# Reordering stage one of a gated attention and mixer block: values' rows loaded later, the first MLP normalisation moved into `w1` of block 3, two of block 3's subtractions on VectorE

## The chip, the cores and the metric

The kernel runs on one core of a Trainium2 chip. The metric is the device time of one execution in microseconds. Engines are named as the profile names them: PE is TensorE's matmul, PEld its weight load, DVE is VectorE, ACT is ScalarE, POOL is GpSimd and SP is SyncE, which does nothing here but issue DMAs. A suffix q (SPq, ACTq) marks the issue of a DMA by that engine's queue.

## The reference

Everything is float32, for one sequence of 2048 tokens of width 448, 16 heads of width 28.

```python
g = sigmoid((x * gate_w).sum(-1, keepdims=True))
a = attention(x, wq, wk, wv, wo)      # 16 query heads of 28, one key and one value head
h  = gelu(layernorm(x) @ w1)          # token mixing, on whole rows
hs = shift(h) @ w2                    # the four quarters of h, moved by -1, +1, -2, +2 tokens
x1 = x + hs
b  = x1 + gelu(layernorm(x1) @ w3) @ w4
out = g * a + (1 - g) * b
```

## The kernel before

The 2048 tokens are four blocks of 512 (`b` = 0 to 3), and a block is four tiles of 128 tokens (`t` = 0 to 3). A float32 product is made of three matmuls on reduced-precision halves: a tensor `raw` is split into a high part (a copy that rounds, on ACT) and a low part (`raw` minus the high part, on DVE or POOL). The kernel has three stages: projections, token mixing and `w2` (stage one, roughly the first 136 us); the channel MLP `w3`, `w4`; attention. The change lies in stage one and moves one small piece to its end.

The order of the work is written out by hand: each engine runs its instructions in the order in which the Python code emits them, and each waits only for its own operands and buffers. So a wait on an engine holds up all that was emitted behind it for that engine. All engines but ACT's few stores leave their DMAs to SP's queue, in that same way in order. A DMA takes one of eight semaphores in turn, and its issue waits until the former user of that semaphore has landed; SP's and ACT's DMAs share the eight.

For one block, stage one does this:

- `stage_w1(b)`: four times 11 matmuls into a PSUM bank of `mm1` (four banks in turn), GELU on ACT into `hf`, a caller's extra work `between(t)`, and a 32x32 transpose on DVE into `ht`. Then SP stores `ht` as `hd` in DRAM with four DMAs.
- `read_h(b)`: two SP DMAs read `hd` back as `hr`, with channels on the partitions (first the quarters 2 and 3, then 0 and 1).
- `split_h(b)`: for the quarters `m` in the order 2, 0, 1, 3, ACT copies `hr` into `hh` and POOL subtracts into `hl`. After quarter 2, `carry_h(b)` issues seven small SP DMAs that move rows of that quarter to the 16 spare partitions of the others. At the end POOL copies the two edge columns into the block before.
- `stage_w2(b)`: per tile 11 matmuls into one of two banks `hs`, then DVE adds the bank to the residual `x1`. With two banks, the third tile's matmuls start when the first tile's addition is done.
- `stage_q(u)`: one group of four query heads; PE projects, ACT copies to `qf` and stores it to `qd` by its own queue. The queries' spare rows hold keys and values as well, so `stage_kv(b)` reads the values' rows of a block from `qd` into `vT` with two SP DMAs. `vT` is used first by `stage_v`, in the middle of `stage_w2(3)`.

The channel MLP needs the normalised block 0: `stats_tile` (DVE) gives mean and variance of a row of `x1`, `stats_end` (POOL) the reciprocal root, `layernorm_norm` (DVE) one subtraction and multiplication into `xn` and a transpose into `xt4`; `xt_write` stores that as `xd` with four SP DMAs, `xt_read` loads it as `xr` with three, and `ln_split` (ACT, then DVE) splits it. `load_w34(i)` loads the raw weights of the channel MLP, two DMAs each.

Three buffers of 8 KB a partition, tag `raw`, serve in turn for `ht`, `hr`, `xn4` and `xt4`. In the kernel before the turn gives `xt4` the buffer that `ht` of block 3 had. The order of the last part of stage one before the change can be read at the end of the functions printed here.

Of the kernel before, what the change touches and what calls it, by code (L numbers as in the profile page):

```python
# [9 lines left out]
F32 = mybir.dt.float32  # L10
F32R = mybir.dt.float32r
AF = mybir.ActivationFunctionType
ALU = mybir.AluOpType
# [3 lines left out]
P = 128  # L17
S = 2048
D = 448
# [4 lines left out]
NB = S // 512  # L24
NT = S // P
NF = F // P
NE = D // 32
# [10 lines left out]
def f32(ap):  # L38
    return ap.bitcast(F32)
# [3 lines left out]
def gated_mix_kernel(  # L43
# [12 lines left out]
    nc = tc.nc  # L56
# [80 lines left out]
    def stats_tile(pool, b, t, mv):  # L137
        st = pool.tile([P, 6], F32, tag="st", bufs=2, name=f"st_{pool.name}_{b}_{t}")
        nc.vector.bn_stats(st, x1[:, 4 * b + t, :])
        nc.vector.bn_aggr(mv[:, t, :], st)  # L140

    def stats_end(mv, rs):
        nc.gpsimd.tensor_tensor(rs, mv[:, :, 1], epst, ALU.add)
        nc.gpsimd.tensor_tensor(rs, rs, powt, ALU.pow)

    def stats_tiles(pool, b):
        return (pool.tile([P, 4, 2], F32, tag="mv", bufs=2, name=f"mv_{pool.name}_{b}"),
                pool.tile([P, 4], F32, tag="rs", bufs=2, name=f"rs_{pool.name}_{b}"))
# [8 lines left out]
    def layernorm_norm(b, t, mv, rs, xn, xt4):  # L157
        xt = x1[:, 4 * b + t, :]
        nc.vector.tensor_scalar(xn, xt, mv[:, t, 0:1], rs[:, t:t + 1], op0=ALU.subtract, op1=ALU.mult)
        nc.vector.transpose(xt4[:, :, t, :], xn.rearrange("p (f j) -> p f j", j=32))  # L160
# [3 lines left out]
    def xt_write(b, xt4):  # L164
        xd_of[b] = dram.tile([NE, 32, 4, 128], F32, tag="xd", bufs=2, name=f"xd_{b}")
        for p in range(4):
            nc.sync.dma_start(xd_of[b][:, :, p].rearrange("f i u -> i f u"),
                              xt4[32 * p:32 * p + 32].rearrange("i f t j -> i f (t j)"))

    def xt_read(b, raw):  # L170
        xd = xd_of.pop(b)
        nc.sync.dma_start(raw[:, 0:3, :], xd[0:12].rearrange("(c f) i p u -> (f i) c (p u)", c=3))
        for k in (0, 64):
            nc.sync.dma_start(raw[k:k + 64, 3, :], xd[12:14].rearrange("f i p u -> (f i) (p u)"))
# [75 lines left out]
    with tc.tile_pool(name="s1b", bufs=1) as s1b, \  # L250
            tc.tile_pool(name="ps1", bufs=1, space=PSUM) as ps1:
        s1_stack = ExitStack()
        s1 = s1_stack.enter_context(tc.tile_pool(name="s1", bufs=1))
        turn = [0]

        def mm1(name):
            k = turn[0] % 4
            turn[0] += 1
            return mm_tile(name) if k < 2 else ps1.tile([P, 512], F32, tag="tp", bufs=2, name=name)
# [62 lines left out]
        def rest(g, n, b):  # L322
            cols = slice(512 * b, 512 * b + 512)
            return qd[g].rearrange("(j c) s -> j c s", c=32)[0:n // 4, DH:32, cols]

        def stage_kv(b):
            for g in range(2):
                at = 32 * b + 16 * g
                nc.sync.dma_start(vT[at:at + 16, :], rest(2 + g, 16, b))
# [69 lines left out]
        def carry_h(b):  # L399
            src = f32(hl[b])  # L400
            for i, (low, m, _) in enumerate(CARRY):
                o = 2 + SHIFTS[m]
                to = f32((hl if low else hh)[b])[C:P, m, o:o + 512]
                nc.sync.dma_start(to, src[16 * i:16 * i + 16, 2, 0:512])  # L404

        hd_of, hr_of = {}, {}

        def stage_w1(b, between=None):
            ah, al = xact[b]
            rs = rs1_of.pop(b)[1]  # L410
            ht = s1.tile([P, 4, 512], F32, tag="raw", bufs=3, name=f"ht_{b}").rearrange("p c n -> p (c n)")
            ht = ht[:, 0:4 * D].rearrange("p (f t j) -> p f t j", f=NE, t=4)
            for t in range(4):
                ps = mm1(f"h_{b}_{t}")[:, 0:D]
                tok = slice(t * P, (t + 1) * P)
                for c in range(3):
                    nc.tensor.matmul(ps, ah[:, c, tok], w1h[:, c, :], start=(c == 0), stop=False)
                    nc.tensor.matmul(ps, al[:, c, tok], w1h[:, c, :], start=False, stop=False)
                    nc.tensor.matmul(ps, ah[:, c, tok], w1l[:, c, :], start=False, stop=False)
                nc.tensor.matmul(ps, ah[:, 3, tok], w1h[:, 3, :], start=False, stop=False)  # L420
                nc.tensor.matmul(ps, ah[:, 3, tok], w1l[:, 3, :], start=False, stop=True)
                hf = s1.tile([P, 512], F32, tag="hf", bufs=3, name=f"hf_{b}_{t}")[:, 0:D]
                nc.scalar.activation(hf, ps, AF.Gelu_apprx_tanh, scale=rs[:, t:t + 1])
                if between:
                    between(t)
                nc.vector.transpose(ht[:, :, t, :], hf.rearrange("p (f j) -> p f j", j=32))
            hd = hd_of[b] = dram.tile([NE, 32, 4, 128], F32, tag="hd", bufs=2, name=f"hd_{b}")
            for p in range(4):
                nc.sync.dma_start(hd[:, :, p].rearrange("f i u -> i f u"),
                                  ht[32 * p:32 * p + 32].rearrange("i f t j -> i f (t j)"))  # L430
# [8 lines left out]
        def split_h(b):  # L439
            hh[b] = s1b.tile([P, 4, 516], F32R, tag="hh", bufs=2, name=f"hh_{b}")  # L440
            hl[b] = s1b.tile([P, 4, 516], F32R, tag="hl", bufs=2, name=f"hl_{b}")
            hr = hr_of.pop(b)
            for tt in (hl, hh):
                if b == 0:
                    nc.gpsimd.memset(f32(tt[b])[0:C, :, 0:2], 0.0)
                else:
                    nc.gpsimd.tensor_copy(tt[b][0:C, :, 0:2], f32(tt[b - 1])[0:C, :, 512:514])
            for m in ORDER:
                raw = hr[0:C, m, :].rearrange("n (p t j) -> n p t j", p=4, t=4)
                hi, lo = [tt[b][0:C, m, 2:514].rearrange("n (t p j) -> n p t j", p=4, t=4) for tt in (hh, hl)]  # L450
                nc.scalar.copy(hi, raw)
                nc.gpsimd.tensor_tensor(lo, raw, f32(hi), ALU.subtract)
                if m == 2:
                    carry_h(b)
            for tt in (hh, hl):
                if b:
                    nc.gpsimd.tensor_copy(tt[b - 1][0:C, :, 514:516], f32(tt[b])[0:C, :, 2:4])
                if b == NB - 1:
                    nc.gpsimd.memset(f32(tt[b])[0:C, :, 514:516], 0.0)

        def stage_w2(b, between=None):
            for t in range(4):
                ps = hs_tile(f"hs_{b}_{t}")[:, 0:D]
                for m in range(4):
                    o = 2 + t * P + SHIFTS[m]
                    nc.tensor.matmul(ps, hh[b][0:C, m, o:o + P], w2h[0:C, m, :], start=(m == 0), stop=False)
                    nc.tensor.matmul(ps, hh[b][:, m, o:o + P], w2l[:, m, :], start=False, stop=False)
                    if m != 2:
                        nc.tensor.matmul(ps, hl[b][:, m, o:o + P], w2h[:, m, :], start=False, stop=(m == 3))
                xt = x1[:, 4 * b + t, :]  # L470
                nc.vector.tensor_add(xt, xt, ps)
                if between:
                    between(t)
# [66 lines left out]
        stage_w1(1, second)  # L540
        split_h(0)
        read_h(1)
        stage_kv(0)
        stage_kv(1)
        stage_w1(2, lambda t: ln1_tile(3, t))
        split_h(1)
        read_h(2)
        stage_kv(2)
        stage_q(12)
        stage_q(13)  # L550
        stage_w2(0)
        mv0, rs0 = stats_tiles(s1, "m")

        def fourth(t):
            if t == 0:
                split_h(2)
            stats_tile(s1, 0, t, mv0)

        stage_w1(3, fourth)
        read_h(3)  # L560
        stats_end(mv0, rs0)
        xn4 = s1.tile([P, 2048], F32, tag="raw", bufs=3, name="xn4")[:, 0:4 * D].rearrange("p (t n) -> p t n", t=4)
        xt4 = s1.tile([P, 2048], F32, tag="raw", bufs=3, name="xt4")[:, 0:4 * D].rearrange(
            "p (f t j) -> p f t j", f=NE, t=4)
        stage_w2(1, lambda t: layernorm_norm(0, t, mv0, rs0, xn4[:, t, :], xt4))
        xt_write(0, xt4)
        split_h(3)
        stage_q(14)
        stage_q(15)
        stage_kv(3)  # L570
        s1_stack.close()

        late = ctx.enter_context(tc.tile_pool(name="late", bufs=1, side="right", reuse_waits="tile"))
# [57 lines left out]
        xraw2[0] = big("xr_0").rearrange("p (c n) -> p c n", c=4)  # L631
        load_w34(0, s2a)
        xt_read(0, xraw2[0])

        def third(t):
            if t == 3:
                ln_split(0, 0, 2)
# [16 lines left out]
    with tc.tile_pool(name="s2", bufs=1, reuse_waits="tile") as s2, \  # L654
# [47 lines left out]
        for b in range(NB):  # L702
            acc = [ps2.tile([P, 512], F32, tag="acc", bufs=4, name=f"acc_{b}_{t}") for t in range(4)]
            gs = {}
            for f in range(NF):
                if f == 9 and b + 1 < NB:
                    mv, rs = layernorm_stats(s2a, b + 1)
                if f == 10 and b + 1 < NB:
                    xt4 = big(f"xt4_{b + 1}")[:, 0:4 * D].rearrange("p (f t j) -> p f t j", f=NE, t=4)
                if f in (10, 11) and b + 1 < NB:  # L710
                    for t in (2 * f - 20, 2 * f - 19):
                        xn = s2a.tile([P, 512], F32, tag="xn", bufs=1, name=f"xn_{b + 1}_{t}")[:, 0:D]
# [474 lines left out]
```

## Time and profile before

| | |
|---|---|
| median of 3 runs | 924.17 us (923.05 to 924.31) |
| the profiled execution's own time | 923.91 us |
| its span, first to last instruction | 922.1 us |
| PE busy in the span | 905.3 us (98%) |
| DVE, ACT, POOL busy | 541.1, 632.2, 107.0 us |
| mean granted TensorE clock | 0.991 of full speed |
| DMA share in slices 3 to 6 of 40 (46 to 138 us) | 6, 5, 6 and 5 tenths |

Times of single instructions below are microseconds from the start of the span. The parts of the page are averages over three stages with different limits; what this change is worth is read from the stretch of 60 to 140 us alone, in the timeline of each engine. In a row of a timeline stand the start, the duration, the engine, the line, the operation, the tiles (buffer numbers left out), and, in brackets, how long the engine had been idle before it and what ended that.

### The profile page before, as it was taken

What the parts mean: (1) busy time and instruction counts of PE and PEld (TensorE: products, weight loads), DVE (VectorE), ACT (ScalarE), POOL (GpSimd) and SP (SyncE); (2) the same over time, 40 slices, a digit from 0 to 9 for tenths busy, and PEclk for the clock granted to TensorE, in tenths of its full rate; (3) what the DMA queues carried; (4) which work ended last, traced back from release to release, by engine and by line L of the source; (5) the groups of instructions that cost most, each with busy time, mean ns of one, the idle gap of its engine ahead of it and who ended that gap; (6) DMA issues with size and microseconds to landing.
All of it is one profiled execution on the core that took longest, in us unless ns stands there. A gap on an engine that the chain in (4) does not pass through costs nothing.

```text
span 922.1 us, 24138 instructions
## 1 busy us (share of the span) xinstructions
PE 905.3 (98%) x10097; PEld 649.7 (70%) x10097; DVE 541.1 (59%) x1083; ACT 632.2 (69%) x1135; POOL 107.0 (12%) x140
## 2 busy tenths in 40 slices
PE   9999879999999999999999999999999999999998
PEld 7898768888888888885556655556655656665554
DVE  4653344542344655536666666676666666666775
ACT  5433135522222122239999999999999999999996
POOL 3134300112100052002200000000000000000000
PEclk9999879999999999999999999999999999999999
DMA  9865654140041141111000001100011000010001
GB/s 302 304 156 146 150 181 129 44 96 22 9 98 36 38 98 52 46 30 59 15 14 25 26 14 44 35 26 26 3 36 56 21 8 26 14 51 18 15 14 43
DMA packets 50608, 58.23 MB, mean 63 GB/s; under 512 B 9616, under 2 KB 35008, under 8 KB 50496
## 3 DMA queue, kind: packets, MB, share of 16 engines
q1 hardware_dynamic: 47328, 50.95, 20.1%
q10 hardware_dynamic: 3168, 5.70, 1.7%
q8 instruction: 80, 1.31, 0.6%
q14 instruction: 32, 0.26, 0.1%
HBM read 39.80 MB, written 15.59 MB: 60 GB/s over the span
## 4 chain that ended last, share of the span: by engine, by line
PE 92%; DMA 3%; DVE 2%; SPq 1%; ACT 1%; issue 1%; POOL 0%; ACTq 0%; DVEq 0%; POOLq 0%
PE bank L985 24%; PE bank L948 22%; PE bank L849 7%; PE acc L699 5%; PE acc L698 5%; PE acc L700 5%; PE g L132 4%; PE g L131 4%; PE g L133 4%; PE g L134 1%; PE g L135 1%; DMA hr<-hd 1%; SPq L404 1%; PE q L309 1%; DMA xr<-xd 1%; PE q L131 1%
## 5 line engine op out<-in xcount | busy, mean ns | idle before, releaser
L975 ACT ACTIVATE p<-bank 128x512 f32<-128x512 f32 x762 | 386.9, 617 | 1.5 <-PE bank L948 1.5
L985 PE MATMUL bank<-p,vext 128*32 128x256 f32 x3076 | 244.4, 379 | 0.0
L985 PE MATMUL bank<-pd,vext 128*32 128x256 f32 x1020 | 241.1, 380 | 0.0
L972 DVE COPY pd<-bank 128x512 f32<-128x512 f32 x254 | 175.3, 692 | 51.2 <-PE bank L948 49.9
L985 PEld LDWEIGHTS bank<-p,vext 128*32 128x32 f32 x3076 | 126.7, 110 | 81.6 <-ACT p L975 0.5
L687 ACT ACTIVATE gh<-g 128x512 fp32r<-128x512 f32 x54 | 32.2, 597 | 183.1 <-PE g L135 183.1
L989 DVE TENSOR_TENSOR o<-o,bank 128x256 f32<-128x256 f32 x222 | 93.5, 421 | 92.1 <-ACT p L975 53.9
L980 ACT ACTIVATE pd<-pd 128x1024 f32<-128x1024 f32 x127 | 141.0, 1110 | 0.0
L948 PE MATMUL bank<-qh,kH 30*128 30x512 f32 x1024 | 116.7, 444 | 0.0
L985 PEld LDWEIGHTS bank<-pd,vext 128*32 128x32 f32 x1020 | 112.4, 110 | 0.1
L690 DVE TENSOR_TENSOR gl<-gf,gh 128x512 fp32r<-128x512 f32 x54 | 37.2, 689 | 119.4 <-ACT gf L688 119.3
L948 PE MATMUL bank<-qh,kL 28*128 28x512 f32 x1024 | 103.8, 391 | 0.0
L948 PE MATMUL bank<-ql,kH 28*128 28x512 f32 x1024 | 103.7, 391 | 0.0
L948 PEld LDWEIGHTS bank<-qh,kH 30*128 30x128 f32 x1024 | 60.4, 183 | 57.2 <-ACT p L975 45.9
L699 PE MATMUL acc<-w4l,gh 128*128 128x448 f32 x216 | 79.0, 366 | 0.0
L698 PE MATMUL acc<-w4h,gh 128*128 128x448 f32 x216 | 78.9, 365 | 0.0
L700 PE MATMUL acc<-w4h,gl 128*128 128x448 f32 x216 | 78.8, 365 | 0.0
L849 PE MATMUL bank<-wof,on 128*32 128x224 f32 x1008 | 73.1, 367 | 0.0
L132 PE MATMUL g<-al,w3h 128*128 128x512 f32 x168 | 65.8, 392 | 0.0
L131 PE MATMUL g<-ah,w3h 128*128 128x512 f32 x168 | 65.7, 391 | 0.0
L133 PE MATMUL g<-ah,w3l 128*128 128x512 f32 x168 | 65.6, 390 | 0.0
L948 PEld LDWEIGHTS bank<-ql,kH 28*128 28x128 f32 x1024 | 50.8, 186 | 9.5
(201 smaller groups left out, 1170.3 us busy)
## 6 DMA issues: line engine op xcount, KB each, us to landing
qd<-qf ACTq DMA_DIRECT2D x16, 256.0 KB
qm<-qd SPq DMA_DIRECT2D x16, 256.0 KB
qr<-qd SPq DMA_DIRECT2D x16, 256.0 KB
rb<-rd SPq DMA_DIRECT2D x15, 256.0 KB
x<-in_x_dram SPq DMA_DIRECT2D x4, 896.0 KB
hd<-ht SPq DMA_DIRECT2D x16, 224.0 KB
hr<-hd SPq DMA_DIRECT2D x8, 448.0 KB
xd<-xt SPq DMA_DIRECT2D x16, 224.0 KB
```

Source lines behind the costliest of these rows:

```text
L131: nc.tensor.matmul(ps, wh[:, c, :], ah[:, c, :], start=(c == 0), stop=False)
L132: nc.tensor.matmul(ps, wh[:, c, :], al[:, c, :], start=False, stop=False)
L133: nc.tensor.matmul(ps, wl[:, c, :], ah[:, c, :], start=False, stop=False)
L698: nc.tensor.matmul(ps, gh[:, tok], w4h[i][:, k, :], start=(f == 0), stop=False)
L699: nc.tensor.matmul(ps, gh[:, tok], w4l[i][:, k, :], start=False, stop=False)
L700: nc.tensor.matmul(ps, gl[:, tok], w4h[i][:, k, :], start=False, stop=(f == stop))
L849: nc.tensor.matmul(ps[32 * j:32 * j + 32, cols], on_of[u][:, tok], wof[:, u % NG, cols], start=start, stop=stop, tile_position=(0, 32 * j))
L948: nc.tensor.matmul(bs[j], w, a, start=(i == 0), stop=(i == 2), tile_position=(32 * j, 0))
L972: nc.vector.tensor_copy(ps[j], bs[j])
L975: behind[kt % 2] = nc.scalar.activation(ps[j], bs[j], AF.Exp, scale=SCALE)
L980: ins = nc.scalar.activation(pd, pd, AF.Exp, scale=SCALE)
L985: nc.tensor.matmul(pv[32 * j:32 * j + 32, q], vext[:, kt, :], p_of[u, kt][j][:, q], start=start, stop=stop, tile_position=(0, 32 * j))
```

## The change

Four things are moved, and one is shared:

- `stage_kv(0)`, `(1)` and `(2)` are issued together behind `read_h(2)`, and `stage_kv(3)` behind `xt_read(0)`.
- The statistics of block 0's rows of `x1` are taken in `stage_w2(0)`, each behind its addition, and not in `stage_w1(3)`.
- The normalisation of block 0 runs in `stage_w1(3)`, ahead of each tile's transpose of `hf`, and not in `stage_w2(1)`. Its `xn` takes buffers of the tag `qf` (four of 2 KB); its `xt4` is allocated together with `ht` of block 3, so that it gets the buffer that `hr` of block 1 had. `xn4` is gone.
- `xt_write(0)` is issued right behind the stores of `hd` of block 3, ahead of `read_h(3)`.
- In `split_h(3)` the subtractions of quarters 0 and 3 run on DVE, those of 2 and 1 stay on POOL.

```diff
-        def stage_w1(b, between=None):
+        def token_tile(b):
+            ht = s1.tile([P, 4, 512], F32, tag="raw", bufs=3, name=f"ht_{b}").rearrange("p c n -> p (c n)")
+            return ht[:, 0:4 * D].rearrange("p (f t j) -> p f t j", f=NE, t=4)
+
+        def stage_w1(b, between=None, ht=None):
...
-                nc.gpsimd.tensor_tensor(lo, raw, f32(hi), ALU.subtract)
+                eng = nc.vector if b == NB - 1 and m in (0, 3) else nc.gpsimd
+                eng.tensor_tensor(lo, raw, f32(hi), ALU.subtract)
...
         read_h(1)
-        stage_kv(0)
-        stage_kv(1)
         stage_w1(2, lambda t: ln1_tile(3, t))
         split_h(1)
         read_h(2)
-        stage_kv(2)
+        for b in range(3):
+            stage_kv(b)
         stage_q(12)
         stage_q(13)
-        stage_w2(0)
         mv0, rs0 = stats_tiles(s1, "m")
+        stage_w2(0, lambda t: stats_tile(s1, 0, t, mv0))
+        stats_end(mv0, rs0)
 
         def fourth(t):
             if t == 0:
                 split_h(2)
-            stats_tile(s1, 0, t, mv0)
-
-        stage_w1(3, fourth)
+            xn = s1.tile([P, 512], F32, tag="qf", bufs=4, name=f"xn_0_{t}")[:, 0:D]
+            layernorm_norm(0, t, mv0, rs0, xn, xt4)
+
+        h3 = token_tile(3)
+        xt4 = token_tile("x")
+        stage_w1(3, fourth, h3)
+        xt_write(0, xt4)
         read_h(3)
-        stats_end(mv0, rs0)
...
-        stage_w2(1, lambda t: layernorm_norm(0, t, mv0, rs0, xn4[:, t, :], xt4))
-        xt_write(0, xt4)
+        stage_w2(1)
         split_h(3)
         stage_q(14)
         stage_q(15)
-        stage_kv(3)
...
         xt_read(0, xraw2[0])
+        stage_kv(3)
```

PE's order does not change. On SP's queue, the first place is the time between the reads of `hr` for blocks 1 and 2 (L329 is `stage_kv`, L429 the store of `hd`, L433 the same line after the change, L437 and L441 `read_h`, L404 the carried rows). Before:

```order
L437 DMA hr_1_605<-hd_1_581 112x2x512 x2
L329 DMA vT_134<-qd_81 16x1x512 x4
L429 DMA hd_2_689<-ht_2_612 32x14x128 x4
L404 DMA hh_1_694<-hl_1_695 16x512 x2
...
L437 DMA hr_2_715<-hd_2_689 112x2x512 x2
L329 DMA vT_134<-qd_81 16x1x512 x2
```

And after:

```order
L441 DMA hr_1_605<-hd_1_581 112x2x512 x2
L433 DMA hd_2_685<-ht_2_608 32x14x128 x4
L404 DMA hh_1_690<-hl_1_691 16x512 x2
...
L441 DMA hr_2_711<-hd_2_685 112x2x512 x2
L329 DMA vT_134<-qd_81 16x1x512 x6
```

Four reads of `vT` no longer stand ahead of block 2's stores; all six now stand behind the read of `hr_2`.

The second place on SP's queue is from block 3's stores to the reads of the normalised rows (L167 stores `xd`, L172 and L174 read it as `xr`, L598 and L599 or L601 and L602 load raw weights of the channel MLP). Before:

```order
L429 DMA hd_3_898<-ht_3_804 32x14x128 x4
L437 DMA hr_3_903<-hd_3_898 112x2x512 x2
L167 DMA xd_0_970<-xt4_909 32x14x128 x4
L404 DMA hh_3_975<-hl_3_976 16x512 x2
...
L329 DMA vT_134<-qd_81 16x1x512 x2
L598 DMA w34raw_0_1050<-in_w3_dram 128x4x256
L599 DMA w34raw_0_1050<-in_w4_dram 128x2x448
L172 DMA xr_0_1045<-xd_0_970 128x3x512
```

And after:

```order
L433 DMA hd_3_913<-ht_3_818 32x14x128 x4
L167 DMA xd_0_918<-ht_x_819 32x14x128 x4
L441 DMA hr_3_923<-hd_3_913 112x2x512 x2
L404 DMA hh_3_978<-hl_3_979 16x512 x2
...
L601 DMA w34raw_0_1051<-in_w3_dram 128x4x256
L602 DMA w34raw_0_1051<-in_w4_dram 128x2x448
L172 DMA xr_0_1046<-xd_0_918 128x3x512
L174 DMA xr_0_1046<-xd_0_918 64x512 x2
L329 DMA vT_134<-qd_81 16x1x512 x2
```

The stores of `xd` went from behind `read_h(3)` to ahead of it, and block 3's `vT` from ahead of the weights to behind `xr`.

On DVE, the place is the end of `stage_w1(3)` and `stage_w2(1)` (L426 or L430 transposes `hf` into `ht`, L471 or L476 adds a bank to `x1`, L159 and L160 are the normalisation and its transpose, L139 and L140 the statistics). Before:

```order
L426 STREAM_TRANSPOSE ht_3_804<-hf_3_2_874 128x14x32
L139 BN_STATS st_s1_0_3_894<-x1_72 128x6
L140 BN_AGGR mv_s1_m_802<-st_s1_0_3_894 128x2
L426 STREAM_TRANSPOSE ht_3_804<-hf_3_3_892 128x14x32
L471 TENSOR_TENSOR x1_72<-x1_72,hs_1_0_910 128x448
L159 TENSOR_SCALAR xn4_908<-x1_72,mv_s1_m_802,rs_s1_m_803 128x448
L160 STREAM_TRANSPOSE xt4_909<-xn4_908 128x14x32
L471 TENSOR_TENSOR x1_72<-x1_72,hs_1_1_925 128x448
```

And after, down to the first addition of block 2 (L457 is the subtraction of `split_h`):

```order
L430 STREAM_TRANSPOSE ht_3_818<-hf_3_2_889 128x14x32
L159 TENSOR_SCALAR xn_0_3_909<-x1_72,mv_s1_m_750,rs_s1_m_751 128x448
L160 STREAM_TRANSPOSE ht_x_819<-xn_0_3_909 128x14x32
L430 STREAM_TRANSPOSE ht_3_818<-hf_3_3_907 128x14x32
L476 TENSOR_TENSOR x1_72<-x1_72,hs_1_0_926 128x448
L476 TENSOR_TENSOR x1_72<-x1_72,hs_1_1_939 128x448
L476 TENSOR_TENSOR x1_72<-x1_72,hs_1_2_952 128x448
L476 TENSOR_TENSOR x1_72<-x1_72,hs_1_3_965 128x448
L457 TENSOR_TENSOR hl_3_979<-hr_3_923,hh_3_978 112x4x4x32 x2
L476 TENSOR_TENSOR x1_72<-x1_72,hs_2_0_1059 128x448
```

The normalisation left the additions of block 1 and stands ahead of the transposes of block 3's `hf`; two subtractions of `split_h(3)` now stand ahead of the additions of block 2.

More of the change, by code (lines that the diff above doesn't have):

```diff
@@ L406, in gated_mix_kernel @@
         hd_of, hr_of = {}, {}
-        def stage_w1(b, between=None):
+        def token_tile(b):
+            ht = s1.tile([P, 4, 512], F32, tag="raw", bufs=3, name=f"ht_{b}").rearrange("p c n -> p (c n)")
+            return ht[:, 0:4 * D].rearrange("p (f t j) -> p f t j", f=NE, t=4)
+        def stage_w1(b, between=None, ht=None):
             ah, al = xact[b]
             rs = rs1_of.pop(b)[1]
-            ht = s1.tile([P, 4, 512], F32, tag="raw", bufs=3, name=f"ht_{b}").rearrange("p c n -> p (c n)")
-            ht = ht[:, 0:4 * D].rearrange("p (f t j) -> p f t j", f=NE, t=4)
+            if ht is None:
+                ht = token_tile(b)
             for t in range(4):
@@ L556, in fourth @@
                 split_h(2)
-            stats_tile(s1, 0, t, mv0)
-        stage_w1(3, fourth)
-        read_h(3)
-        stats_end(mv0, rs0)
-        xn4 = s1.tile([P, 2048], F32, tag="raw", bufs=3, name="xn4")[:, 0:4 * D].rearrange("p (t n) -> p t n", t=4)
-        xt4 = s1.tile([P, 2048], F32, tag="raw", bufs=3, name="xt4")[:, 0:4 * D].rearrange(
-            "p (f t j) -> p f t j", f=NE, t=4)
-        stage_w2(1, lambda t: layernorm_norm(0, t, mv0, rs0, xn4[:, t, :], xt4))
-        xt_write(0, xt4)
+            xn = s1.tile([P, 512], F32, tag="qf", bufs=4, name=f"xn_0_{t}")[:, 0:D]
[4 more added lines that the diff above has]
+        xt_write(0, xt4)
+        read_h(3)
+        stage_w2(1)
         split_h(3)
```

## The prediction

> **What bounds it now.** I read the page's first part, then PE's waits over the whole span, then clock and load in short stretches.
>
> ```profile
> PE 905.3 (98%) x10097; PEld 649.7 (70%) x10097; DVE 541.1 (59%) x1083; ACT 632.2 (69%) x1135; POOL 107.0 (12%) x140
> PE hs L466 <- DVE x L471: 11.2, 3, 6.1
> 92.00:96.00 4.00, 3.08 (x10) 2.77 (x11) 1.38 (x3) 0.00 (x0) 1.13 (x2) 0.72 0.74 134
> 96.00:100.00 4.00, 0.82 (x4) 0.21 (x2) 1.26 (x3) 0.00 (x0) 0.00 (x0) 0.86 0.56 119
> 100.00:104.00 4.00, 4.00 (x12) 3.57 (x13) 2.54 (x6) 0.33 (x1) 0.00 (x0) 0.57 0.79 222
> 104.00:108.00 4.00, 4.00 (x19) 3.26 (x19) 2.38 (x3) 2.47 (x5) 3.95 (x6) 1.00 0.17 31
> 124.00:128.00 4.00, 0.00 (x0) 0.00 (x0) 1.18 (x2) 1.83 (x4) 0.00 (x0) 0.56 0.42 123
> 128.00:132.00 4.00, 3.29 (x9) 2.99 (x10) 3.94 (x10) 2.73 (x5) 0.00 (x0) 0.50 0.13 15
> ```
>
> PE is the bound, and nearly all it ever waits for is one thing, 11.2 us in three gaps: DVE's addition of a `hs` bank to `x1`, all in stage one. The stretches (PE, PEld, DVE, ACT, POOL busy, granted clock, DMA share, GB/s) show that each gap is followed by a clock near 0.5. The gaps, from PE's timeline:
>
> ```profile
> 92.92 0.48 PE L466 MATMUL hs<-w2h,hh 112*128 112x448 f32 x1 [1.92 <-DVE x L471]
> 99.95 0.48 PE L466 MATMUL hs<-w2h,hh 112*128 112x448 f32 x1 [3.18 <-DVE x L471]
> 128.71 0.74 PE L466 MATMUL hs<-w2h,hh 112*128 112x448 f32 x1 [6.11 <-DVE x L471]
> 136.48 0.39 PE L131 MATMUL g<-ah,w3h 128*128 128x512 f32 x1
> ```
>
> The first two are tiles 2 and 3 of `stage_w2(1)`, the last is tile 2 of `stage_w2(3)`; 7.8 us after that, at 136.48, the channel MLP begins. What DVE did then:
>
> ```profile
> 91.75 0.61 DVE L426 STREAM_TRANSPOSE ht<-hf 128x448 f32<-128x448 f32 x1
> 92.29 0.58 DVE L471 TENSOR_TENSOR x<-x,hs 128x448 f32<-128x448 f32 x1
> 98.74 0.65 DVE L160 STREAM_TRANSPOSE xt<-xn 128x448 f32<-128x448 f32 x1 [4.99 <-DMA hd<-ht]
> 126.82 1.29 DVE L627 TENSOR_TENSOR al<-xr,ah 128x512 fp32r<-128x512 f32 x2 [8.09 <-ACT ah L624]
> 128.03 0.62 DVE L471 TENSOR_TENSOR x<-x,hs 128x448 f32<-128x448 f32 x1
> ```
>
> Gap two: the first normalised tile must wait until block 3's `ht` has left the buffer, and the next addition stands behind it. Gap three: the addition stands behind `ln_split`, which waits for `xr`. So I follow the chain of waits and SP's queue back from 128.71:
>
> ```profile
> 74.52 4.64 DMA qd<-qf
> 119.15 7.00 DMA xr<-xd
> 126.17 0.63 ACT ah L624
> 69.86 3.19 SPq L429 DMA_DIRECT2D hd<-ht  x4
> 81.06 1.02 SPq L437 DMA_DIRECT2D hr<-hd  x2
> 92.39 3.03 SPq L429 DMA_DIRECT2D hd<-ht  x4
> 98.76 0.81 SPq L437 DMA_DIRECT2D hr<-hd  x2
> 106.44 3.75 SPq L167 DMA_DIRECT2D xd<-xt  x4
> 110.31 2.73 SPq L404 DMA_DIRECT2D hh<-hl  x2
> 114.35 1.22 SPq L404 DMA_DIRECT2D hh<-hl  x2
> 117.78 0.61 SPq L598 DMA_DIRECT2D w34raw<-in_w_dram  x1
> ```
>
> The end of stage one is one queue: stores of `hd` at 92.39, read at 98.76, then the stores of `xd`, which could not go before 106.44, the carried rows behind them, weights at 117.78, `xr` at 119.15. From the weights' issue to PE's restart is 128.71 - 117.78 = 10.9 us. **My sum is the new time of that weights' issue**, with the 10.9 us behind it unchanged.
>
> **The change, part by part.**
>
> *Values' rows.* Block 2's `ht` was complete when its stores waited behind four reads of `vT`:
>
> ```profile
> 66.29 0.61 DVE L426 STREAM_TRANSPOSE ht<-hf 128x448 f32<-128x448 f32 x1
> 66.88 2.87 SPq L329 DMA_DIRECT2D vT<-qd  x4
> 85.44 0.62 ACT L451 CAST hh<-hr 112x512 fp32r<-112x512 f32 x1 [5.06 <-DMA hr<-hd]
> 86.97 1.68 ACT L451 CAST hh<-hr 112x512 fp32r<-112x512 f32 x3 [0.91 <-DMA hr<-hd]
> 88.55 1.67 ACT L423 ACTIVATE hf<-h,rs_s 128x448 f32<-128x448 f32 x3
> ```
>
> They go 3.0 us earlier (66.9 for 69.86). Block 2's read is not simply 3.0 us earlier: the carried rows ahead of it take over semaphores of the two `qd` stores, the second of which landed at 74.52 + 4.64 = 79.16, with the `hd` stores still in flight beside it. Those will be further along, so the `qd` store should land sooner: by nothing (4.64 stays) or by the full 3.0 us (1.64). I take the middle, 77.6; two carried rows at 0.61 (1.22 for two at 114.35) follow, and the read issues near 78.9 instead of 81.06: 2.2 us earlier, between 0.7 and 3.2. The six reads of `vT` behind it (0.72 each, 4.3 us) end near 84.3. The next carried rows wait for POOL's first subtraction of block 2, near 85, so they cost nothing; without that cover each would be 0.72. `vT` is used 30 us later.
>
> *Statistics* go behind additions that come one in 2.26 us, with DVE idle 1.64 between:
>
> ```profile
> 113.59 0.62 DVE L471 TENSOR_TENSOR x<-x,hs 128x448 f32<-128x448 f32 x1 [1.64 <-PE hs L469]
> 115.85 0.62 DVE L471 TENSOR_TENSOR x<-x,hs 128x448 f32<-128x448 f32 x1 [1.64 <-PE hs L469]
> 101.42 0.50 DVE L159 TENSOR_SCALAR xn<-x,mv_s_m,rs_s_m 128x448 f32<-128x448 f32 x1
> 104.37 4.46 POOL L452 TENSOR_TENSOR hl<-hr,hh 112x512 fp32r<-112x512 f32 x4
> 104.53 1.20 DVE L159 TENSOR_SCALAR xn<-x,mv_s_m,rs_s_m 128x448 f32<-128x448 f32 x1
> 87.67 3.26 POOL L452 TENSOR_TENSOR hl<-hr,hh 112x512 fp32r<-112x512 f32 x3 [0.43 <-ACT hh L451]
> ```
>
> They are free.
>
> *Normalisation in `w1` of block 3.* ACT's next GELU there was at 88.55, behind block 2's copies; 2.2 us earlier is 86.4. Its result reaches DVE 0.65 us later (87.0). Tiles 0 and 1 are normalised by then. What remains in order is transpose, `xn`, `xt`, transpose, `xn`, `xt`, transpose: three by 0.61, two by 0.50, two by 0.65, together 4.1, so about 91.0 overlapped as issued. One `xn` meets POOL's subtractions of block 2 (87.67 less 2.2, until 88.7): under such a one it took 1.20 for 0.50, which I price at 0.7. So `ht` is complete at 91.7, for 92.39: only 0.7 earlier, as the 2.2 go to four DVE instructions that used to stand behind. The Trainium skill, "SBUF — State Buffer", section "SBUF: two separate sides", has DVE and POOL share one port pair as an exclusive lock for a whole instruction; the 1.20 agrees. By it the two subtractions given to DVE would also take turns with POOL's rather than run beside them, so the sharing would buy less than it seems; the weights' issue would stay where I put it.
>
> The additions of block 1 then follow each other with nothing between. PE restarts 0.63 behind the start of an addition (92.92 less 92.29), so at 92.3, 1.3 us after it stopped at 91.0; gap two, 3.18 us, is gone. Tile 2 took 3.85 us at the slow clock (92.92 to 96.77); then, from 96.2, comes what PE did from 99.95 to 122.60, 22.6 us. Its first two tiles of `w2(3)` are done at 118.8, less up to 1.7 if the clock holds (0.43 of the 4 us at 0.57).
>
> *Stores of `xd` before the read of block 3.* From stores to read was 98.76 - 92.39 = 6.4 us; four more issues (3.75 at most) fit inside. The read issues at 98.1. To its landing: alone 85.44 - 81.06 = 4.4 us, 102.5. With the 0.9 MB of `xd` moved first: the `hd` stores used (0.74 + 0.56) x 4 = 5.2 us of DMA time, twice that from about 92.5 is 103, and with 2.5 of the read's 4.4 us behind it (an estimate) 105.5. I take 103.6, nearer to the first because the second counts all traffic there as `hd`.
>
> *Block 3's split.* ACT's copy 0.62, POOL's subtraction 1.1 (4.46 for four): 105.3. The second half of the read lands 1.5 later (86.97 less 85.44), ACT's last three copies take 1.68, DVE's last subtraction 0.65 (1.29 for two) and up to 1.1 for POOL: 107.4 to 108.5. Behind it stands the first addition of block 2, which PE wants by 109.1 (118.8 less four tiles of 2.26 and 0.63): nothing lost, by 0.6 us at the worst.
>
> *Carried rows and weights.* Seven at 0.61 give 4.3: weights at 109.6, for 117.78. They used to take 5.9 with landings of `xd` awaited, which are now old. `vT` of block 3 (2 x 0.72) is moved past them, 1.4 us that are in the old 117.78. It is wanted by PE only a tile after the restart.
>
> *Sum:* 117.78 - 109.6 = 8.2 us. PE restarts at 120.5, 1.7 us after it is ready at 118.8, and the 7.8 us to the first `g`, slow clock in them, I leave as they are. 923.91 - 8.2 = 915.7 against the profiled execution, which lies 0.26 below the median of 924.17. Bounds: the late `qd` adds 1.5, the late landing 1.9 (to 919.1); the early ones take off 2.6, but PE's own 118.8 allows 1.7: 914.0.
>
> **The rivals.**
>
> *Stores in the way.* `xd` is wholly served ahead of block 3's read, and block 2's read gains little: weights at 109.6 + 1.9 + 1.5 = 113.0, a gain of 4.8, and up to 1.5 less if `qd` 14 and 15 crowd the weights: 919 to 921. For it: share 0.74 at only 134 GB/s with `hd` alone. Against: the second window falls to 0.56, so the engines have room. The Trainium skill's "DMA: Bandwidth & Descriptors", section "Queues, rings and completion order", says that each DMA engine consumes a ring's descriptors in order, which speaks for this rival; no row here shows two such stores in a row.
>
> *PE becomes the bound again.* If the clock holds and `xr` lands by 114.6, gap three closes: PE goes on at 117.1 instead of 128.71, 11.6 us, and without a slow clock behind it up to 2.0 more (half of the 4 us at 0.50): 910.3 to 912.3. It needs the early bound in both places and a quicker chain besides.
>
> *No change.* The weights are issued at 109.6, but `xr` arrives as late as before, held by traffic: 923.9. Weights and `xr` took 126.17 - 117.78 = 8.4 us; they would have to take 16.6, and the only newcomers are two `qd` stores of 256 KB.
>
> *Slower.* DVE's two subtractions now stand ahead of block 2's additions, and they wait for block 3's read. If that lands after 111.8, POOL's subtraction ends after 113.5 and the weights go after 117.78: PE loses in two places. That is 13.7 us after the issue, against 4.4. At 119 GB/s, the worst row, 1.84 MB take 15 us from 92, still 109.7; so it needs a slower DMA than any row. Price 2 to 3 us: 926.5.
>
> **How the numbers follow.** Forecast (912 to 918.5) 0.58, stores in the way 0.17, PE-bound 0.12, no change 0.06, slower 0.07. This kernel's runs can tell about 0.2%, 1.8 us: faster 0.87, same 0.06, slower 0.07. The forecast, most of the second and half of the third make 0.8: 910.5 to 920.5.
>
> **What would show it.** Right: PE's second wait for `x` is gone; `xd` stores near 95; the weights' issue near 109.6; a last gap of 1 to 4 us. Wrong: `hr` of block 3 landing past 106; ACT's copies of block 2 still near 85; the longest PE gap moving into `stage_w2(2)`, behind DVE's subtractions.

## The result and the profile after

| | before | after |
|---|---|---|
| median (lowest to highest, 4 runs each) | 923.87 us (923.05 to 924.31) | 917.76 us (917.10 to 918.45) |
| profiled execution, and its span | 923.91, 922.1 us | 917.57, 915.7 us |
| PE busy; PE's wait for `x1` | 905.3; 11.2 us | 902.7; 7.3 us |

The ratio is 0.9935 (95% interval 0.9918 to 0.9952): 6.1 us faster, where 8.2 were forecast. The two lines of PE account for the span's 6.4 us: 3.9 us less waiting, and 2.6 us less time for the same matmuls, because fewer of them ran at a slow clock. (PE's busy time times the missing share of the clock, over the stretches of 4 us from 92 to 136, comes to 5.7 us before and 2.9 after; this is an estimate.)

First the same views as before: busy time from the page, PE's wait, PE's gaps in its timeline with the first `g`, and stretches of 4 us (PE, PEld, DVE, ACT, POOL busy, granted clock, DMA share, GB/s).

```profile
PE 902.7 (99%) x10097; PEld 648.2 (71%) x10097; DVE 543.7 (59%) x1085; ACT 632.1 (69%) x1135; POOL 105.3 (12%) x138
PE hs L471 <- DVE x L476: 7.3, 3, 2.9
93.60 0.53 PE L471 MATMUL hs<-w2h,hh 112*128 112x448 f32 x1 [2.14 <-DVE x L476]
111.63 0.47 PE L471 MATMUL hs<-w2h,hh 112*128 112x448 f32 x1 [2.22 <-DVE x L476]
123.86 0.47 PE L471 MATMUL hs<-w2h,hh 112*128 112x448 f32 x1 [2.92 <-DVE x L476]
130.46 0.39 PE L131 MATMUL g<-ah,w3h 128*128 128x512 f32 x1
92.00:96.00 4.00, 2.40 (x7) 2.18 (x8) 2.07 (x4) 0.00 (x0) 0.00 (x0) 0.74 0.54 96
96.00:100.00 4.00, 4.00 (x18) 3.62 (x18) 0.66 (x2) 0.00 (x0) 0.00 (x0) 0.84 0.99 215
100.00:104.00 4.00, 4.00 (x19) 3.34 (x18) 0.58 (x1) 0.00 (x0) 0.32 (x2) 1.00 0.95 222
112.00:116.00 4.00, 4.00 (x21) 3.69 (x20) 0.73 (x2) 0.00 (x0) 0.53 (x3) 1.00 0.52 140
124.00:128.00 4.00, 4.00 (x14) 3.50 (x15) 3.94 (x8) 1.89 (x4) 0.00 (x0) 0.58 0.27 69
```

The middle gap (3.18 us in `stage_w2(1)`) is gone. A new one of 2.22 us stands in `stage_w2(2)`, the last fell from 6.11 to 2.92, and the first `g` comes at 130.46 for 136.48: 6.0 of the span's 6.4 us are gained ahead of that point.

Now the chain behind the last gap: SP's waits in 60 to 120 us, and SP's, ACT's, POOL's and DVE's timelines.

```profile
SPq L404 <- DMA qd<-qf: 3.8, 1, 3.8
73.48 4.88 SPq L404 DMA_DIRECT2D hl<-hl  x2
80.36 1.03 SPq L441 DMA_DIRECT2D hr<-hd  x2
84.67 0.63 ACT L455 CAST hh<-hr 112x512 fp32r<-112x512 f32 x1 [3.85 <-DMA hr<-hd]
86.73 3.24 POOL L457 TENSOR_TENSOR hl<-hr,hh 112x512 fp32r<-112x512 f32 x3 [0.24 <-ACT hh L455]
88.83 1.40 DVE L159 TENSOR_SCALAR xn<-x,mv_s_m,rs_s_m 128x448 f32<-128x448 f32 x1
93.06 3.03 SPq L433 DMA_DIRECT2D hd<-ht  x4
96.14 4.57 SPq L167 DMA_DIRECT2D xd<-ht_x  x4
100.89 1.84 SPq L441 DMA_DIRECT2D hr<-hd  x2
107.14 0.62 ACT L455 CAST hh<-hr 112x512 fp32r<-112x512 f32 x1 [17.86 <-DMA hr<-hd]
107.84 1.12 POOL L457 TENSOR_TENSOR hl<-hr,hh 112x512 fp32r<-112x512 f32 x1 [7.48 <-ACT hh L455]
113.48 0.62 SPq L601 DMA_DIRECT2D w34raw<-in_w_dram  x1
121.33 2.18 ACT L627 CAST ah<-xr 128x512 fp32r<-128x512 f32 x4 [9.99 <-DMA xr<-xd]
```

The weights' issue, on which the sum was built, moved from 117.78 to 113.48 and not to 109.6. Between block 3's stores at 93.06 and the copy of its `hr` at 107.14 lie 14.1 us, of which four stores of `xd` on the same queue and the traffic they make are the new part.

### The profile page after: what moved, and what is told of

It reads as the page before. It is cut to its first block, busy times and chain, and to the rows that moved or that the text cites. A ratio compares the mean times of both kernels' runs of the same rounds, so it can differ in the third digit from the quotient of the medians.

```text
span 915.7 us, 24147 instructions
## 1 busy us (share of the span) xinstructions
PE 902.7 (99%) x10097; PEld 648.2 (71%) x10097; DVE 543.7 (59%) x1085; ACT 632.1 (69%) x1135; POOL 105.3 (12%) x138
## 4 chain that ended last, share of the span: by engine, by line
PE 91%; DMA 3%; SPq 2%; DVE 2%; ACT 1%; POOL 1%; issue 1%; ACTq 0%; DVEq 0%; POOLq 0%
PE bank L989 24%; PE bank L952 22%; PE bank L853 7%; PE acc L703 5%; PE acc L702 5%; PE acc L704 5%; PE g L132 4%; PE g L131 4%; PE g L133 4%; DMA hr<-hd 2%; PE g L134 1%; PE g L135 1%; SPq L404 1%; PE q L309 1%; POOL hl L457 1%; DMA xr<-xd 1%
## 5 line engine op out<-in xcount | busy, mean ns | idle before, releaser
L703 PE MATMUL acc<-w4l,gh 128*128 128x448 f32 x216 | 78.9, 365 | 0.0
```

The source lines that it names most:

```text
L703: nc.tensor.matmul(ps, gh[:, tok], w4l[i][:, k, :], start=False, stop=False)
```

## The experiments

All are edits of the changed kernel, except where the text says otherwise. Kernels were run in three sets, each beside the kernel before on the same chip (924.48, 925.14 and 924.27 us there), and are compared by their ratio to it. The changed kernel's ratio, from a set of its own, is 0.9935; the expectations were written with its 917.8 us in mind. The ratios on record differ from those of the medians by up to about 0.001, or 1 us.

Single executions differ even ahead of everything that was edited: block 0's stores of `hd` issue at 46.9 in both main profiles, and between 46.8 and 47.7 in those of the variants. A row that moves by less than 0.8 us therefore shows little by itself.

The theory after the result: the chain from block 2's read to the weights sets the end, and `xd`, put ahead of block 3's read, costs part of what its early place brings. The rival: the order on SP does not matter, and something else does.

**The order of `xd` and the read.**

```diff
-        xt_write(0, xt4)
         read_h(3)
+        xt_write(0, xt4)
```

> The changed kernel with the four stores of xd issued behind the read of block 3's hr instead of ahead of it; nothing else. Theory (stores in the way): the read issues when hd has landed, 6.4 us after the first hd store (99.5 instead of 100.9), and lands 4.4 us later (103.9 instead of 107.1), so POOL's first subtraction of block 3 ends 3.2 us earlier; some of that is lost again, as the carried rows must await the landings of xd. The weights' issue moves from 113.5 to 110.5 to 112, the whole from 917.8 to 914.8 to 916.5. Rival (the read is late because DMA is full or slow there anyway): the read lands at 106 to 107 as now, the time stays within 1 us of 917.8.

Measured: 918.47 us, ratio 0.9927 (0.9914 to 0.9940): the same time as the changed kernel. SP's and POOL's timelines in this variant, and SP's waits in 96 to 120 us:

```profile
99.60 0.81 SPq L441 DMA_DIRECT2D hr<-hd  x2
104.36 1.11 POOL L457 TENSOR_TENSOR hl<-hr,hh 112x512 fp32r<-112x512 f32 x1 [5.36 <-ACT hh L455]
110.72 1.20 SPq L404 DMA_DIRECT2D hh<-hl  x2
112.67 0.62 SPq L601 DMA_DIRECT2D w34raw<-in_w_dram  x1
SPq L404 <- DMA qd<-qf: 2.2, 2, 2.0
```

The theory's mechanism is there and its time, 914.8 to 916.5, is not. The read issues 1.3 us earlier and POOL subtracts 3.5 us earlier (104.36 for 107.84). But the seven carried rows now take from 105.50 to 112.6, where 4.3 us would do: the fifth (110.72) and the sixth wait 2.2 us for the two `qd` stores of `stage_q(14)` and `(15)`, whose semaphores they take in this order of DMAs, and the fourth waits 0.4 us for `xd`. The weights gain 0.8 us, and `xr`, behind them, takes that back (ACT copies it at 121.56, for 121.33); why it takes longer is not shown. The execution in the trace took 919.3 us, and the six lie between 916.5 and 919.4. The rival named the right time and a wrong reason, since the read did not land late. So in this trace the read does pay for `xd`, and most of the gain from moving it was stopped at the next wait on SP.

**SP's time or the transfers?** The four stores of `xd` on ACT's queue:

```diff
-            nc.sync.dma_start(xd_of[b]...
+            (nc.sync if b else nc.scalar).dma_start(xd_of[b]...
```

> The changed kernel with the four stores of xd issued by ACT's queue at the same place in the program; nothing else. This parts the issue on SP from the transfer. If the time on SP's queue is what delays the read (4.6 us for four stores), the read issues at 99.5 and lands within 4.4 to 5 us, near 104, and the time is 915 to 916. If the transfer of 0.9 MB beside it is what delays it, the read issues at 99.5 but lands at 106 to 107 as now, and the time stays at 917 to 918. If the landing of hd is also delayed by the stores, the read issues at 101 or later: 918 to 919.

Measured: 919.15 us, ratio 0.9931 (0.9918 to 0.9944): the same. From SP's and ACT's timelines:

```profile
93.73 5.13 SPq L433 DMA_DIRECT2D hd<-ht  x4
93.21 3.80 ACTq L167 DMA_DIRECT2D xd<-ht_x  x4
104.60 1.14 SPq L441 DMA_DIRECT2D hr<-hd  x2
108.27 0.62 ACT L455 CAST hh<-hr 112x512 fp32r<-112x512 f32 x1 [18.33 <-DMA hr<-hd]
```

SP is free of `xd`, and yet the read issues 3.7 us later, since it needs `hd` landed (SP waits 5.5 us for that) and the two sets of stores now share the engines: `hd`'s four issues take 5.13 us for 3.03, and the read goes 10.9 us behind the first of them, for 7.8. It then lands quicker, so that the copy on ACT comes 14.5 us behind the first store of `hd`, for 14.1. So it is the transfers that cost: taking the issues off SP brought nothing while both sets were in flight. Of the three cases expected, the trace shows the last (the read at 101 or later), with the time of the second. The Trainium skill, "DMA: Bandwidth & Descriptors", section "Queues, rings and completion order", says that each DMA engine goes round the queue rows that have work, packet by packet. That two sets on two queues slowed each other agrees with it; no row here shows turns by packet.

**The normalisation ahead of the transposes.** All four `xn` and `xt` while DVE is idle:

```diff
-            layernorm_norm(0, t, ...)
+            for n in ((0, 1), (2, 3), (), ())[t]:
+                layernorm_norm(0, n, ...)
```

> The changed kernel with all four tiles of the normalisation emitted ahead of the second transpose of hf, in the 4.6 us in which DVE idles, instead of one ahead of each transpose. Theory (normalisation and the port that it shares with POOL hold up ht): no xn lasts longer than 0.55 us (1.40 for one now), ht is complete at about 90.5 instead of 93.0, hd's first store issues at 91.3, then held by the seven carried rows of block 2 that SP issues until 91.3; the chain is 1.8 us shorter: 916.0 (915.3 to 916.8). The gap of PE in tile 2 of w2 of block 1, 2.14 us, is gone. Rival (the carried rows or the read set the time, not ht): time as it is, 917.8 within 0.8.

Measured: 916.3 us, ratio 0.9902 (0.9889 to 0.9916), just below the changed kernel's interval (from 0.9918). No `xn` takes over 0.51 us, the three last transposes follow each other, and block 3's stores go 1.1 us earlier.

```profile
88.75 1.70 DVE L430 STREAM_TRANSPOSE ht<-hf 128x448 f32<-128x448 f32 x3 [2.33 <-ACT hf L427]
91.94 3.23 SPq L433 DMA_DIRECT2D hd<-ht  x4
112.23 0.62 SPq L602 DMA_DIRECT2D w34raw<-in_w_dram  x1
129.23 0.39 PE L131 MATMUL g<-ah,w3h 128*128 128x512 f32 x1
```

The 1.2 us of the weights are 1.2 us at the first `g`, so this place is on the path, as the theory had it. Its 1.8 us did not come in full: `ht` is complete at 90.45, but SP issues block 2's carried rows until 91.84, and only then the stores. PE's first gap is gone, and the one in `stage_w2(2)` grew to 4.45 us, as PE comes there earlier.

**Is the sharing with DVE on the path?**

```diff
-                eng = nc.vector if b == NB - 1 and m in (0, 3) else nc.gpsimd
+                eng = nc.gpsimd
```

> The changed kernel with all four subtractions of block 3 on POOL; nothing else. Theory (the sharing is off the path, and its wait on DVE costs a gap that a later wait takes back): the gap of 2.2 us at 111.6 goes, as block 2's first addition no longer stands behind DVE's subtractions, POOL ends its fourth near 112.4, the weights still issue at 113.5 behind the carried rows, and the last gap grows from 2.9 to about 5: 917.8 within 1. Rival (the sharing is what makes block 3 early): POOL's later end moves the weights by 1 us or more and the time is 919 or more. Second rival (the gap in w2 of block 2 is on the path): 915.6.

Measured: 917.9 us, ratio 0.9932 (0.9919 to 0.9945): the same. From PE's timeline:

```profile
112.17 0.47 PE L471 MATMUL hs<-w2h,hh 112*128 112x448 f32 x1 [0.37 <-POOL hh L464]
123.65 0.74 PE L471 MATMUL hs<-w2h,hh 112*128 112x448 f32 x1 [5.05 <-DVE x L476]
130.45 0.39 PE L131 MATMUL g<-ah,w3h 128*128 128x512 f32 x1
```

The 2.22 us in `stage_w2(2)` are indeed DVE's subtractions, and without them PE waits as much longer at the next gap. The sharing neither brought nor cost anything here.

**The values' rows, undone and alone.**

```diff
         read_h(1)
+        stage_kv(0)
+        stage_kv(1)
         stage_w1(2, ...)
...
         read_h(2)
-        for b in range(3):
-            stage_kv(b)
+        stage_kv(2)
```

> The changed kernel with the values' rows of blocks 0 and 1 read ahead of w1 of block 2 and those of block 2 behind read_h(2), as before; block 3's stay behind xr. Theory: the later reads gave block 2's read of hr only 0.7 us (80.4 for 81.1), as the semaphore of the second qd store holds it in both orders; undone, the read is at 81 again, ht of block 3 and the chain behind it 0.3 to 0.9 us later: 918.1 to 918.8. Rival (the forecast's 2.2 us, partly hidden): 919.5 to 920. Second rival: nothing, 917.8.

Measured: 920.11 us, ratio 0.9948 (0.9934 to 0.9961). Block 2's read goes at 81.33 for 80.36, block 3's stores at 93.92 for 93.06, the weights at 114.46 for 113.48. Of these 0.9 to 1.0 us, 0.3 were there ahead of the edit (block 1's read at 66.00 for 65.73), which leaves 0.6 to 0.7, the theory's size, though no more than single executions differ by. The ratio is 1.2 us above the changed kernel's, between the theory's 0.3 to 1.0 and the rival's 1.7 to 2.2; the two intervals overlap, so the times alone prove neither. The counterpart is the kernel before with this move alone (the diff reversed):

> The kernel before with the values' rows alone moved: all six reads of vT behind the read of block 2. Theory: the carried rows still wait for the second qd store, so block 2's read goes 0.7 us earlier and not 2.2, and hd of block 3, its read and the weights follow by 0.7 to 1.0 us: 0.7 to 1.2 us faster than the kernel before on this chip (the other undoing, without this move, lost about 1.2). Rival, the prediction's step as written: the read goes 2.2 us earlier, which makes 2 us or a little more. Second rival: DVE's normalisation in w2(1) sets that end, and nothing is gained.

Measured: 923.29 us against 924.27, ratio 0.9987 (0.9978 to 0.9996), 1.0 us. The forecast's 2.2 us would be 0.9976, just outside the interval. Where that 1.0 us lies is not shown. In the profiled execution (924.21 us, among the slowest of its eleven) block 2's read is 0.6 us and block 3's 0.3 us earlier, but the weights come 0.8 us later (118.55): behind the read, the issues of `xd` and of the carried rows start later and take longer.

**`xr` ahead of the weights.**

```diff
-        load_w34(0, s2a)
         xt_read(0, xraw2[0])
+        load_w34(0, s2a)
```

> The changed kernel with xt_read(0) ahead of load_w34(0); nothing else. It takes the two weight loads (1.3 us of issue, 0.96 MB) from in front of xr. Theory (the 10.4 us from the weights' issue to PE's restart are mostly issue and transfer ahead of xr): xr lands 3 to 4 us earlier, 117.5 to 118.5 instead of 121.3; PE, ready at about 120.9, has no last gap and no slow clock behind it, and the first g, 130.5 now, is bounded by PE's own work or by the weights' halves: 126.5 to 128. Time 914 to 916. Rival (xr waits for something else, such as the first qd store's semaphore): xr at 121, time 917.8.

Measured: 915.3 us, ratio 0.9897 (0.9883 to 0.9912). From ACT's and PE's timelines:

```profile
118.81 2.19 ACT L627 CAST ah<-xr 128x512 fp32r<-128x512 f32 x4 [7.44 <-DMA xr<-xd]
127.28 0.39 PE L131 MATMUL g<-ah,w3h 128*128 128x512 f32 x1
```

`xr` is copied 2.5 us earlier and the last gap is gone; the first `g` comes 3.2 us earlier. The gap in `stage_w2(2)` is longer, 3.84 us, as PE comes there earlier, but it ends where it did (111.65 for 111.63). The two loads of weights, 1 MB, had been in front of the transfer that PE waited for.

**`xd` out of the way.** On top of the early normalisation, `xd` stored at once, and the carried rows of block 2 taken out of `split_h(2)` and issued behind block 3's stores:

```diff
+            if t == 1:
+                xt_write(0, xt4)
...
         stage_w1(3, fourth, h3)
-        xt_write(0, xt4)
+        carry_h(2)
         read_h(3)
```

> The changed kernel with all four tiles normalised ahead of the second transpose of hf, the stores of xd issued right then (about 86.5) and the carried rows of block 2 behind the stores of hd instead of ahead. Theory (the transfer of xd between hd's stores and block 3's read is what the forecast missed: 3.5 us, and ht's lateness 1.5): xd goes at 86.5 to 90.3 while DMA is mostly idle, hd at 90.5, the carried rows in the wait for hd's landing, the read at 97.5 to 98, landing at 102 to 102.5, weights at 108.5 to 109.5, xr at 116.5 to 117.5; time 912.5 to 914. Rival (the transfer of xd costs the same wherever it stands): hd lands late, the read issues at 100 or later, 916 to 918.

Measured: 914.2 us, ratio 0.9883 (0.9868 to 0.9898). SP's, ACT's and PE's timelines:

```profile
85.86 3.07 SPq L167 DMA_DIRECT2D xd<-ht_x  x4
89.68 3.98 SPq L433 DMA_DIRECT2D hd<-ht  x4
98.77 1.03 SPq L441 DMA_DIRECT2D hr<-hd  x2
102.81 0.62 ACT L455 CAST hh<-hr 112x512 fp32r<-112x512 f32 x1 [13.83 <-PE hs L474]
109.14 0.62 SPq L604 DMA_DIRECT2D w34raw<-in_w_dram  x1
108.38 0.48 PE L471 MATMUL hs<-w2h,hh 112*128 112x448 f32 x1 [3.33 <-DVE x L476]
```

The read now stands behind block 2's carried rows, and issues 9.1 us after the first store of `hd`. But ACT copies `hr` at 102.81, at most 4.0 us behind the read's issue, for 6.3 in the changed kernel, and the carried rows of block 3 run unheld (4.3 us): the weights go at 109.14, near the 109.6 that the prediction had for the changed kernel. That is the best evidence here that `xd` in flight around the read is what the prediction underpriced. It is not a clean one: the early normalisation and the carried rows moved too. Against the early normalisation alone the first `g` comes 2.3 us earlier (126.95 for 129.23), and the intervals of those two ratios overlap.

**Both, and then the sharing again.** The last variant with `xr` first:

> The kernel with early xd, and xt_read(0) ahead of load_w34(0). Theory (both cuts lie on the same chain and add until PE is the bound): xr lands at 113 to 114.5, PE goes on without the last gap, the first g at 124 to 126, time 911 to 913. Rival (the weights' landing then holds the first g): 913 to 914, as with early xd alone.

Measured: 912.5 us, ratio 0.9868 (0.9853 to 0.9883). PE's timeline has one gap left before the first `g`:

```profile
108.82 0.74 PE L471 MATMUL hs<-w2h,hh 112*128 112x448 f32 x1 [3.27 <-DVE x L476]
124.37 0.39 PE L131 MATMUL g<-ah,w3h 128*128 128x512 f32 x1
```

What is left is the wait behind DVE's two subtractions. So they were put back on POOL, on top of the rest:

> All four edits of the fastest variant so far (912.5 us), and block 3's four subtractions on POOL again. Theory: with xr early, the only gap left on PE is the 3.27 us in w2(2) behind DVE's two subtractions, and it is now on the path. POOL starts at about 103.9, takes 4.45 us for the four (a little more, as quarter 3 is copied late) and 1.2 us for the edge columns, so the fourth tile of w2(2), which needs the edges, starts near 109.8 where PE would want it at 108.3: a gap of about 1.5 us in place of 3.27, so 910.5 us, 909.5 to 911.3. Rival: the gap is off the path, as it was in the kernel under study, where a later one took up its loss: 912.5 us again.

Measured: 910.71 us, ratio 0.9851 (0.9836 to 0.9866), as the theory said. The trace is less clear:

```profile
109.19 0.47 PE L471 MATMUL hs<-w2h,hh 112*128 112x448 f32 x1 [1.34 <-POOL hh L464]
118.09 0.74 PE L471 MATMUL hs<-w2h,hh 112*128 112x448 f32 x1 [2.48 <-DVE x L476]
```

The gap fell from 3.27 to 1.34 us (1.5 was expected), but in this execution, at 912.4 us the slowest of its four, PE ran into `xr` again, and the first `g`, at 124.47, is no earlier. The two ratios' intervals overlap: that this variant beats the one before it is likely, not shown. Both beat the changed kernel by 5 us and more, and neither is beaten by any other variant run.

Of the change's 6.1 us, these runs put nothing that can be seen on the sharing or on the order of `xd` and the read, and about 1 us on the values' rows of blocks 0 to 2. The other 5 us are left to the normalisation in `w1` and to block 3's values' rows. The first lets the stores of `xd` go 10.3 us earlier (96.14 for 106.44) and closes the gap in `stage_w2(1)`; the second takes 1.4 us of issue from ahead of the weights. No run undoes either alone, so their shares are a remainder and not measured.

## Why the prediction was right, and where it was short

The time (917.76) lies in the forecast's range (912 to 918.5), 2.1 us above the point, and the path was the right one. The sum's terms, from the two profiled executions:

| term | forecast | measured | late by |
|---|---|---|---|
| block 3's `ht` complete, stores issue | 91.7 | 93.06 | 1.4 |
| from there to the read's issue | 6.4 | 7.8 | 1.4 |
| to ACT's copy of `hr` | 5.5 | 6.3 | 0.8 |
| to the weights' issue | 6.0 | 6.3 | 0.3 |
| weights to PE's restart | 10.9 | 10.4 | -0.5 |
| restart to the first `g` | 7.8 | 6.6 | -1.2 |

3.9 us were lost up to the weights and 1.7 given back behind them: 2.2 us short of 8.2, which leaves the 6.0 us at the first `g`. The 1.7 us are luck, since the sum left both of these terms as they were; without them the gain would have been 4.3 us, in the range of the rival with the stores in the way.

- *Values' rows.* The mis-sized term was the landing of the `qd` stores and what follows it. I let the second store land sooner by half of the 3.0 us, at 77.6, and counted two carried rows behind it. There are three, as these rows of the kernel before show, so my own landing gives 79.5 for the read, and not 78.9:

```profile
79.19 1.14 SPq L404 DMA_DIRECT2D hh<-hl  x2
80.37 0.59 SPq L404 DMA_DIRECT2D hl<-hl  x1
```

After the change the first of the two stores held SP, by the semaphore that the fourth row waits for: 3.8 us, until about 77.8, with that row and three more still to go. So block 2's read gained 0.7 us and not 2.2. That is the number of the lower bound, but not by its reasoning. ACT's copy went at 84.67, near the 85 that the text had named as the sign of being wrong, and its next GELU at 87.60 for 86.4. With the next point this makes the 1.4 us in the first line.

- *Normalisation in `w1`.* Right in kind: one `xn` met POOL and took 1.40 for 0.47 us, where 0.7 extra was priced and 0.9 came. As GELU came late, block 3's stores went 0.7 us later than in the kernel before, not 0.7 earlier. That this stretch is on the path is shown by the variant that clears it.
- *`xd` ahead of the read.* "Four more issues fit inside" is the step that failed. By the sum's own rows they do not fit: the stores of `hd` take 3.03 of the 6.4 us, and 3.75 more end 0.4 us past them. The four took 4.57 us, for the 3.75 at most that I took from a place with less traffic, and the read stood behind them. It landed past 106, the other sign named. DMA share and rate (0.99 and 0.95 at 215 and 222 GB/s in 96 to 104) show the engines full; I had read the second window's 0.56 as room.
- *Block 3's split and PE's gaps.* "Nothing lost" behind DVE's subtractions was wrong by 2.2 us in `stage_w2(2)`, because the read landed late, but right in effect: the last gap took it in, as the run with POOL alone shows. The second gap is gone as said.
- *Carried rows* were right: 4.3 us, unheld.
- *Behind the restart* I left the slow clock as it was. It lasted one stretch after the change (0.58, then 1.00), and longer before it (0.50, then 0.66), which fits the 1.2 us: by these rows about 1.7 us were lost after and 3.0 before. My sentence that each gap is followed by a clock near 0.5 does not fit its own first row, 0.72. The second stretches, of after and then of before:

```profile
128.00:132.00 4.00, 4.00 (x21) 3.59 (x20) 2.15 (x7) 2.33 (x4) 0.56 (x2) 1.00 1.02 340
```

```profile
132.00:136.00 4.00, 4.00 (x17) 3.60 (x16) 2.45 (x5) 1.69 (x4) 0.00 (x0) 0.66 0.96 320
```

Of the rivals, "stores in the way" came true as a mechanism: weights at 113.48, where it had 113.0. Its time, 919 to 921, did not, as it left the last two terms unchanged too. "PE becomes the bound", "no change" and "slower" did not occur.

## What to carry to other kernels

When a store is moved ahead of a critical read on one queue, price it with the engines at full load, and ask what each later transfer must wait for: here the read paid for 0.9 MB of stores ahead of it, turning the two around let the next wait on the queue take most of the gain, and what paid was moving the stores out of the window, together with an earlier normalisation. A wait that is hidden by a later one (the sharing with DVE) shows neither gain nor loss until that later one is gone; try it again then. Where several transfers go to one consumer stage, issue first the one that an engine stands still for: `xr` ahead of 1 MB of weights moved the first `g` by 3.2 us.

## What the hardware showed beside this

DVE's work stretched under POOL's in two kinds of instructions: `xn` 1.40 us for 0.47 above, and one of the two subtractions given to it, beside POOL's second one (109.36, 1.14 us), in DVE's timeline of the changed kernel:

```profile
108.86 0.69 DVE L457 TENSOR_TENSOR hl<-hr,hh 112x512 fp32r<-112x512 f32 x1 [8.28 <-ACT hh L455]
109.83 1.22 DVE L457 TENSOR_TENSOR hl<-hr,hh 112x512 fp32r<-112x512 f32 x1 [0.28 <-ACT hh L455]
```

The first overlapped POOL's two (107.84 to 108.96 and from 109.36) by 0.3 us in all and took 0.69; the second, with 0.67 us of POOL's second beside it, took 1.22 and ended 0.55 behind it. The second fits the taking of turns that the prediction weighed; the first, with little overlap, was not longer for it.

Between about 2 and 3.3 us, a gap's length does not tell whether a slow clock follows. The stretches behind a gap of 3.33 us (the variant with `xd` early) and of 3.27 us (with `xr` first as well):

```profile
108.00:112.00 4.00, 3.62 (x18) 3.33 (x19) 1.48 (x3) 0.03 (x1) 1.22 (x6) 1.00 0.63 195
108.00:112.00 4.00, 3.18 (x9) 2.83 (x10) 1.30 (x3) 0.47 (x1) 1.61 (x8) 0.58 0.77 211
```

One ran on at 1.00 and one at 0.58. In the changed kernel gaps of 2.14 and 2.92 us were followed by 0.74 and 0.58, and one of 2.22 us by 1.00. All seven gaps of 3.8 us and more between 60 and 142 us of these profiles were followed by a stretch at 0.50 to 0.59. So a gap costs its length and, at times, up to half of the next 4 us and a part of the 4 behind those (0.50, then 0.66 above). The Trainium skill, "TensorE: Matmul & The Clock Gate", section "Part 1: The HAM clock gate", speaks of a free-running window, which would explain that equal gaps end differently; where the window lay is not seen here.
